# Batch 1's first transform stage in four tiled bursts, its x loads reordered behind the weight scaling, and the swapped-half products moved by 0.8 steps

## The chip, the cores and the metric

One core of a Trainium2 chip runs the whole kernel. The metric is the device time of one execution in microseconds. The kernel before takes 777.56 us (median of three runs, 776.34 to 777.86).

## The reference

```python
def _attn_ref(x, filt_r, filt_i):                 # x: (8, 3008, 256)
    X = np.fft.rfft(x, axis=1)
    Y = X * (filt_r + 1j * filt_i)[None]          # filters: (1505, 256)
    return np.fft.irfft(Y, n=x.shape[1], axis=1)

def _moe_ref(x, w_in, w_out, alpha):              # x: (24064, 256), d_ff 2048
    h = x @ w_in
    g = h + np.sin(alpha * h) ** 2 / (alpha + 1e-09)
    return g @ w_out
```

Each of eight batches is filtered along its 3008 positions with a Fourier transform, and all 24,064 rows then go through a two-layer network with the activation h + sin(alpha h)^2 / alpha.

## The kernel before

**The transform.** 3008 is factored as 47 x 64, and each batch (a `Spectral` object) goes through four matmul stages. The first stage makes 24 complex frequencies of the 47-point transform. A batch's x comes in four pieces (`load_x`, ch 0 to 3), cast to fp16 by the DMA. The results are copied out of PSUM into `t1_h`, stored to DRAM (`d1`, SP queue) and read back turned (`load_t2`, g 0 to 3, GpSimd queue). `forward` (u 0 to 11) multiplies by the table `d_t`, the copy `xf` is made on ScalarE, and the two partition halves of `xf` are swapped into `xs` by two DMAs. `product` multiplies `xf` by the real part of the filter, and `cross` multiplies `xs` by the imaginary part and adds it; both are on VectorE. `inverse` or `inverse_tiled` is the third stage, and `last` the fourth, which leaves the batch in `y`, ready to be the moving operand of the network. Batch 0 has its own code ahead of the main loop; its last pieces (`last_0`) are spread between the matmuls of the main loop.

**Two forms of the first stage.** Batch 1 uses `first(i)`, sixteen matmuls of 94 rows by 512 columns, one PSUM bank each from the pool `fps` (two banks). Batches 2 to 7 use `first_tiled(ch)`: eight matmuls of 47 rows with 64 output columns, which share the array four at a time, fill two banks of `fps` and two of `hps` (four banks, shared with the network's first layer), and are copied out by two passes on ScalarE and two on VectorE. Such a group of eight is called a burst here. `inverse_tiled(w)` is a burst too, of sixteen matmuls.

**The network.** The positions go through in 48 chunks of 512 (the sixth of every twelve has 384). `hidden(k, jb)` makes one tile: two matmuls into one bank of `hps` (line 601), a cosine on ScalarE (line 605), and one combining pass on VectorE that frees the bank (line 606). `project(k, u)` is eight matmuls of 256 columns (line 621) on chunk k's finished tiles; two such halves complete 128 output rows, and every 256 rows are copied by ScalarE to `o` (line 630) and stored by several DMAs from the GpSimd queue (line 665).

**What sets the order.** The program order on every engine is written out by hand. The main loop runs in steps: step s issues two hidden tiles of one chunk, then `slot(s)`, then one or none or two `project` halves of the chunk before, then `slot(s + 0.5)`. `put(at, fn)` lists a piece of transform work with the step it is due at, and a slot runs everything that is due. So a piece due at 8.5 runs after step 8's projection, and one due at 48.3 runs in slot 48.5. Chunk 0 is projected in steps 8 to 15, and its second half of output rows is copied and stored after step 15's projection. `clear` moves forward and last pieces away from a burst, and `aside` moves a product or cross that is due up to 1.1 steps before a burst to just behind it; both know the bursts from the list `bursts`. A DMA that is put in a slot is issued by its engine's queue in this order, and an issue that waits holds everything behind it on that queue.

```python
    def slot(at):
        run = 0
        while pending and pending[0][0] <= at:
            if pending[0][2]:
                if run and pending[0][0] > at - 1:
                    break
                run += 1
            _, _, _, fn, args = pending.pop(0)
            fn(*args)
```

**GpSimd's own work at the start.** It scales the weights: `weights_in` (six pieces, line 542) and `weights_out` (three, line 574), with batch 1's x loads between them (line 168).

Of the kernel before, what the change touches and what calls it, by code (L numbers as in the profile page):

```python
# [10 lines left out]
FP32 = mybir.dt.float32  # L11
# [7 lines left out]
B, S, C = 8, 3008, 256  # L19
# [4 lines left out]
NK = 4 * NS  # L24
FUSED = 1
TILED = 2
# [45 lines left out]
def kernel(  # L72
# [10 lines left out]
    nc = tc.nc  # L83
# [15 lines left out]
    def after(ins, other):  # L99

        tc.add_manual_dep(ins.ins, other.ins.name, mybir.DependencyInfo(
            mybir.DependencyClass.Sync, mybir.DependencyReason.DATA), reason="order of loads")

    def pool(name, bufs, space=None):
        kw = {} if space is None else {"space": space}
        return ctx.enter_context(tc.tile_pool(name=name, bufs=bufs, **kw))
# [11 lines left out]
    fps = pool("fps", 2, PSUM)  # L118
# [3 lines left out]
    wf_t = cpool.tile([NR, NK], FP16)  # L122
    wt_t = cpool.tile([128, 64], FP16)
    wh_t = cpool.tile([NK, NR], FP16)
    t1_h = [cpool.tile([128, 16, C], FP16, name=f"t1_h{i}") for i in range(2)]
# [13 lines left out]
    for h in range(2):  # L139
        nc.sync.dma_start(out=x32[:, 4 * C * h:4 * C * h + 4 * C],  # L140
                          in_=bass.AP(tensor=x.tensor, offset=x.offset + 4 * h * C, ap=[[32 * C, 96], [1, 4 * C]]))
# [12 lines left out]
    marks = {}  # L154

    def load_x(b, ch):
        xt = xpool.tile([128, 8, C], FP16, name=f"x_{b}_{ch}", tag="x")
        if b >= TILED:
            for h in range(2):
                ins = nc.gpsimd.dma_start(  # L160
                    out=xt[64 * h:64 * h + N1],
                    in_=bass.AP(tensor=x.tensor, offset=x.offset + (b * S + 32 * h + ch * 8) * C,
                                ap=[[64 * C, N1], [1, 8 * C]]))
                after(ins, marks["snake"])
            return xt
        xt = xt[0:NR]
        for n0, n in [(0, 8)] if b or ch < 3 else [(0, 4), (4, 4)]:
            ins = nc.gpsimd.dma_start(
                out=xt[:, n0:n0 + n],
                in_=bass.AP(tensor=x.tensor, offset=x.offset + (b * S + ch * 8 + n0) * C,  # L170
                            ap=[[32 * C, NR], [C, n], [1, C]]),
            )
        if b == 0:
            marks["x", ch] = ins
        if b == 1:
            marks["x1", ch] = ins
            after(ins, marks["w_in"])
        return xt

    flip = [0]  # L180
# [1 line left out]
    def evac(dst, src, on_act=None):  # L182
        flip[0] = (flip[0] + 1) % 3
        if flip[0] if on_act is None else on_act:
            marks["act"] = nc.scalar.copy(out=dst, in_=src)  # L185
        else:
            marks["dve"] = nc.vector.tensor_copy(out=dst, in_=src)  # L187

    class Spectral:
# [10 lines left out]
        def load_x(self, ch):  # L200
            self.x[ch] = load_x(self.b, ch)

        def first(self, i):
            ch, j = divmod(i, 4)
            ps = fps.tile([128, 512], FP32, name=f"pa_{self.b}_{i}", tag="f")
            marks["pe"] = nc.tensor.matmul(out=ps[0:NK, :], lhsT=wf_t, rhs=self.x[ch][:, 2 * j:2 * j + 2, :],  # L206
                                           start=True, stop=True)
            r0 = 8 * (ch % 2)
            evac(t1_h[ch // 2][0:NK, r0 + 2 * j:r0 + 2 * j + 2, :], ps[0:NK, :])
            if j == 3:  # L210
                nc.sync.dma_start(out=self.d1_rows[:, 8 * ch:8 * ch + 8, :], 
                                  in_=t1_h[ch // 2][0:NK, r0:r0 + 8, :])

        def first_tiled(self, ch):
            r0 = 8 * (ch % 2)
            for q in range(2):
                own, tag = (hps, "h") if q else (fps, "f")
                ps = [own.tile([128, 512], FP32, name=f"pa_{self.b}_{ch}_{q}_{h}", tag=tag) for h in range(2)]
                for h in range(2):
                    for c in range(2):  # L220
                        n = 4 * c + 2 * q
                        nc.tensor.matmul(out=ps[h][64 * c:64 * c + 64, :], lhsT=wt_t[64 * h:64 * h + N1],  # L222
                                         rhs=self.x[ch][64 * h:64 * h + N1, n:n + 2, :], start=True, stop=True)
                for h in range(2):
                    evac(t1_h[ch // 2][:, r0 + 4 * h + 2 * q:r0 + 4 * h + 2 * q + 2, :], ps[h], h == 0)
            d1 = self.d1.rearrange("a (h n) c -> a h (n c)", h=2)
            for c in range(2):
                n0 = (8 * ch + 4 * c) * C
                nc.sync.dma_start(out=d1[:, :, n0:n0 + 4 * C],
                                  in_=t1_h[ch // 2][64 * c:64 * c + 2 * NS, r0:r0 + 8, :]  # L230
                                  .rearrange("a (h n) c -> a h (n c)", h=2))
# [125 lines left out]
    for g in range(2):  # L357
        gs = slice(12 * g, 12 * g + 12)
        for k, filt in enumerate((filt_r, filt_i)):
            for q in range(2):  # L360
                if (g, k, q) == (0, 1, 1):
                    split_alpha()
                off, step = ((12 * g) * C, C) if q == 0 else ((N1 - 12 * g) * C, -C)
                marks["filt", g, k] = nc.gpsimd.dma_start(
                    out=f_t[k][64 * k + 32 * q:64 * k + 32 * q + 32, gs, :],
                    in_=bass.AP(tensor=filt.tensor, offset=filt.offset + off,
                                ap=[[N1 * C, 32], [step, 12], [1, C]]))
# [88 lines left out]
    for i in range(16):  # L456
        own, tag = (fps, "f") if i % 3 == 2 else (hps, "h")
        ps = own.tile([128, 512], FP32, name=f"pa_0_{i}", tag=tag)
        nc.tensor.matmul(out=ps, lhsT=wf0_t[0:NR], rhs=x0[i // 4][:, 2 * (i % 4):2 * (i % 4) + 2, :],  # L459
                         start=True, stop=True)  # L460
# [60 lines left out]
    for g in range(6):  # L521
        own, tag = (t2pool, "t2") if g < 3 else (gpool, "g")
# [3 lines left out]
        ins = nc.sync.dma_start(out=w_in32[g][1], in_=w_in_v[:, :, js])  # L526
# [8 lines left out]
    for jb in range(0, 16, 8):  # L535
        ins = nc.sync.dma_start(out=w_out32[:, jb:jb + 8],
                                in_=moe_w_out[128 * jb:128 * jb + 1024].rearrange("(b p) c -> p b c", p=128))
    s1 = Spectral(1)
# [37 lines left out]

    spread_alpha(2)
    spread_alpha(3)
    for step in ([(weights_in, g) for g in range(3)] + [(s1.load_x, 0), (weights_in, 3), (s1.load_x, 1),
                 (weights_in, 4), (s1.load_x, 2), (weights_in, 5), (s1.load_x, 3)]  # L580
                 + [(weights_out, jb) for jb in (0, 4, 8)]):
        step[0](*step[1:])
    warm_pe(12)
    last_0(0, 4)
# [86 lines left out]
    def put(at, fn, *args, pe=False):  # L671
        pending.append((at, len(pending), pe, fn, args))

    def firsts(b):

        return {2: (37.5, 39.5, 41.5, 43.5), 3: (49.5, 54.5, 60.5, 66.5)}.get(
            b, [48 * b - 105.5 + 8 * ch for ch in range(4)])

    def inverses(b):

        return (63.5, 73.5, 81.5) if b == 2 else [48 * b - 46.5 + 16 * w for w in range(3)]

    bursts = [at for b in range(TILED, B) for at in (*firsts(b), *inverses(b))]

    def clear(at):

# [2 lines left out]
    def aside(at):  # L689

        return next((s + 0.05 for s in bursts if s - 1.1 < at <= s), at)
# [4 lines left out]
    for jb in range(12, 16):  # L696
        put(5 + 0.5 * (jb - 12), weights_out, jb, 1)

    for n0, n, at in ((6, 5, 1.5), (11, 4, 11), (15, 4, 13), (19, 4, 15.5), (23, 4, 17), (27, 5, 19)):
        put(at, last_0, n0, n, fps, "f", True)  # L700
    for b in range(1, B):
        s = s1 if b == 1 else Spectral(b)
        z = 48 * b
        if b > 1:
            for ch in range(4):
                put(22 + 4 * ch if b == 2 else firsts(b)[ch] - 8, s.load_x, ch)
        if b < TILED:
            for i in range(16):
                put(6.9 + 0.35 * i, s.first, i, pe=True)
        else:  # L710
            for ch in range(4):
                put(firsts(b)[ch], s.first_tiled, ch, pe=True)
        for g in range(4):
            put(12.5 if b == 1 else 45 if b == 2 else max(70, z - 77 + 12 * g), s.load_t2, g)
        for u in range(12):
            inv = 24 + 1.21 * u if b == 1 else 57 + 2.2 * u if b == 2 else z - 59 + 4 * u
            fwd = inv - 6
            fwd = clear(fwd)
            put(fwd, s.forward, u, pe=True)
            put(aside(fwd + (0.5 if b == 1 else 1.5)), s.product, u)  # L720
            if s.fused:
                put(aside(fwd + (4 if b == 1 else 4.5)), s.cross, u)
            if b < TILED:
                put(inv, s.inverse, u, pe=True)
        if b >= TILED:
            for w in range(3):
                put(inverses(b)[w], s.inverse_tiled, w, pe=True)
        for ch in range(4):
            put(z - (9.5 if b == 1 and ch < 3 else (10.5, 10.5, 10.5, 3)[ch]), s.load_t4, ch)
        for u in range(16):  # L730
            put(clear(z + (u - (5 if b == 1 else 6.5) if u < 4 else 2 * u - 9 if b == 1 else 2.6 * u - 11)),
                s.last, u, pe=True)
# [15 lines left out]
    step = 0  # L748
# [43 lines left out]
```

## Time and profile before

| What | Value |
|---|---|
| Median of three runs | 777.56 us (776.34 to 777.86) |
| The profiled execution's own time | 774.94 us |
| Its span, first to last instruction | 773.2 us |
| TensorE busy, matmuls | 762.8 us, 99% |
| VectorE busy | 658.5 us, 85% |
| ScalarE busy | 610.5 us, 79% |
| GpSimd busy | 370.2 us, 48% |
| Combining passes (line 606) | 768, 672 ns each |
| Cosines (line 605) | 768, 599 ns each |
| Copies of first-stage results on VectorE (128x512 and other forms) | 52, 683 ns each |
| Network first layer, 512 columns (line 601) | 1536, 375 ns each |
| Network second layer, 256 columns (line 621) | 3008, 273 ns each |

The duration of a matmul is its own latency; the matmuls overlap, so what one costs is the distance between the starts of two that follow each other. An engine's idle time is followed in the profile by the one that ended it. The names in the profile leave out the buffer numbers: `ph` is a hidden tile's bank, `v` its combined result, `po` a projection, `pa` a first-stage bank, `pb` a forward, `pc` an inverse, `pd` a last stage, `t<-d` is `load_t2`.

### The profile page before, as it was taken

Reading aid. Unit: us, or ns where it says so; the run is one execution under the profiler, and the core shown is the slowest. Engines: PE = TensorE matmul, PEld = TensorE weight load, DVE = VectorE, ACT = ScalarE, POOL = GpSimd, SP = SyncE. Lnnn points to the kernel's source line nnn. Section 1 sums busy time; section 2 is a strip of 40 time slices with the busy share of each in tenths; the row PEclk is TensorE's granted clock in tenths of the full one; section 3 lists DMA queues with packets and bytes.
Section 4 is the critical chain, followed back from the end, with each engine's and each line's share of the span. In section 5 each row is a group of like instructions: output and inputs, shape, how many; then the busy total and the mean of one; then the engine's idle time right before and its main releaser. Section 6 shows DMA issues by size and latency. Waiting matters only on the chain.

```text
span 773.2 us, 17230 instructions
## 1 busy us (share of the span) xinstructions
PE 762.8 (99%) x6039; PEld 517.1 (67%) x6039; DVE 658.5 (85%) x1174; ACT 610.5 (79%) x1204; POOL 370.2 (48%) x649
## 2 busy tenths in 40 slices
PE   8999999999999999999999999999999999999997
PEld 4757766666666666666666666766666666766666
DVE  7886998999989888898889988899888888777774
ACT  6798887898788878888778787888778777777763
POOL 6455455644646555555565647554554645330000
PEclk9999999999999999999999999999999999999999
DMA  9955678854855438554574536764254322511112
GB/s 227 286 104 165 140 161 249 216 138 109 216 143 137 117 71 222 139 119 120 114 200 110 140 93 151 198 149 121 72 146 106 92 70 55 138 45 34 40 36 62
DMA packets 81518, 101.49 MB, mean 131 GB/s; under 512 B 18884, under 2 KB 60864, under 8 KB 81431
## 3 DMA queue, kind: packets, MB, share of 16 engines
q0 software_dynamic: 27440, 47.29, 26.2%
q1 hardware_dynamic: 53503, 52.84, 25.7%
q8 instruction: 47, 0.77, 0.4%
q14 instruction: 40, 0.33, 0.1%
q10 hardware_dynamic: 488, 0.27, 0.1%
HBM read 56.15 MB, written 46.66 MB: 133 GB/s over the span
## 4 chain that ended last, share of the span: by engine, by line
PE 92%; DVE 5%; ACT 1%; issue 1%; DMA 1%; DVEq 0%
PE po L621 41%; PE ph L601 40%; DVE v L606 3%; PE pd L316 2%; PE pb L243 2%; PE pa L222 2%; PE pc L293 1%; PE pc L513 1%; ACT cos_all L605 1%; PE warm L437 1%; PE pb L491 1%; DMA cos_all<-in_x_dram 1%; PE pa L206 0%; PE pd L403 0%; PE pa L459 0%
## 5 line engine op out<-in xcount | busy, mean ns | idle before, releaser
L606 DVE SCALAR_TENSOR_TENSOR v<-cos_all,ph 128x512 f16<-128x512 f32 (+1 forms) x768 | 483.0, 672 | 95.6 <-ACT cos_all L605 92.0
L605 ACT ACTIVATE cos_all<-ph 128x512 f32<-128x512 f32 (+1 forms) x768 | 413.7, 599 | 99.5 <-PE ph L601 98.9
L665 POOL DMA_DIRECT2D out_dram<-o x530 | 291.7, 556 | 244.8 <-ACT o L630 213.5
L601 PE MATMUL ph<-y,w 128*128 128x512 f16 (+1 forms) x1536 | 389.1, 375 | 1.3 <-DVE v L606 1.1
L621 PE MATMUL po<-w,v 128*128 128x256 f16 x3008 | 389.4, 273 | 0.0
L621 PEld LDWEIGHTS <-v 128*128 128x128 f16 x3008 | 290.0, 98 | 84.2 <-issue 1.0
L601 PEld LDWEIGHTS <-w 128*128 128x128 f16 x1536 | 143.1, 98 | 114.0 <-issue 19.1
L630 ACT COPY o<-po 128x512 f32<-128x512 f32 (+1 forms) x95 | 56.1, 590 | 7.8 <-PE po L621 7.5
L246 ACT CAST xf<-pb 128x512 f16<-128x512 f32 x84 | 50.9, 606 | 1.6 <-PE pb L243 0.8
L185 ACT CAST y<-pd 128x376 f16<-128x376 f32 (+1 forms) x86 | 41.9, 490 | 12.2 <-PE pd L316 8.8
L160 POOL DMA_DIRECT2D x<-in_x_dram x48 | 25.6, 538 | 39.4 <-DVE v L606 29.7
L185 ACT CAST t_h<-pa 128x512 f16<-128x512 f32 (+1 forms) x60 | 32.8, 589 | 12.5 <-PE pa L222 11.3
L316 PEld LDWEIGHTS <-t_a 96*128 96x128 f16 x448 | 31.4, 97 | 12.7
L264 DVE TENSOR_TENSOR p<-p,xs 128x512 f16<-128x512 f16 x84 | 35.7, 425 | 2.9
L263 DVE TENSOR_TENSOR xs<-xs,filt_t 128x512 f16<-128x512 f16 x84 | 35.2, 419 | 1.8 <-DMA xs<-xf 1.6
L257 DVE TENSOR_TENSOR p<-xf,filt_t 128x512 f16<-128x512 f16 x84 | 35.1, 419 | 0.0
L185 ACT CAST gt<-pc 128x512 f16<-128x512 f32 x54 | 28.1, 594 | 8.4 <-PE pc L293 8.4
L187 DVE CAST t_h<-pa 128x512 f16<-128x512 f32 (+1 forms) x52 | 33.5, 683 | 0.1
L243 PE MATMUL pb<-t,d_t 128*128 128x256 f16 x168 | 32.1, 273 | 0.0
L316 PE MATMUL pd<-wh_t,t_a 96*128 96x94 f16 x384 | 31.8, 204 | 0.0
L235 POOL DMA_DIRECT2D t<-d x28 | 24.4, 874 | 11.2 <-DMA d<-t_h 10.1
L243 PEld LDWEIGHTS <-d_t 128*128 128x128 f16 x168 | 16.3, 98 | 14.3
(70 smaller groups left out, 276.9 us busy)
## 6 DMA issues: line engine op xcount, KB each, us to landing
t<-d POOLq DMA_DIRECT2D x28, 384.0 KB, 5.2
xs<-xf SPq DMA_DIRECT2D x168, 64.0 KB
t_a<-d SPq DMA_DIRECT2D x28, 384.0 KB
x<-in_x_dram POOLq DMA_DIRECT2D x50, 188.0 KB, 4.8
d<-t_h SPq DMA_DIRECT2D x48, 192.0 KB
d<-gt SPq DMA_DIRECT2D x36, 256.0 KB
out_dram<-o POOLq DMA_DIRECT2D x91, 64.0 KB, 2.1
out_dram<-o POOLq DMA_DIRECT2D x31, 80.0 KB, 3.4
```

The source lines that it names most:

```text
L185: marks["act"] = nc.scalar.copy(out=dst, in_=src)
L243: nc.tensor.matmul(out=ps[:, i, :], lhsT=d_t[:, s, :], rhs=self.t2[s // 6][:, s % 6, :], start=True, stop=True)
L246: nc.scalar.copy(out=self.xf[u], in_=ps)
L263: nc.vector.tensor_tensor(out=xs, in0=xs, in1=f_t[1][:, 2 * u:2 * u + 2, :], op=ALU.mult)
L264: nc.vector.tensor_tensor(out=p, in0=p, in1=xs, op=ALU.add)
L316: nc.tensor.matmul(out=psv[:, i, :], rhs=wi_t if self.b < TILED else wh_t, start=True, stop=True, lhsT=t4_h[ch // 2][0:NK, n0 % 16 + i, cb ...
L601: nc.tensor.matmul(out=ps[:, 0:n], lhsT=w1[:, cb, jb * 128:jb * 128 + 128], rhs=y_cols[:, cb, c0:c0 + n], start=(cb == 0), stop=(cb == 1))
L605: nc.scalar.activation(out=cs[:, 0:n], in_=ps[:, 0:n], func=AFT.Sin, bias=float(np.pi / 2))
L606: marks["snake"] = nc.vector.scalar_tensor_tensor(out=v[k][:, jb, 0:n], in0=cs[:, 0:n], scalar=-1.0, in1=ps[:, 0:n], op0=ALU.add, op1=ALU. ...
L621: nc.tensor.matmul(out=pso[k][:, t % 2, :], lhsT=v[k][:, jb, 128 * t:128 * t + 128], rhs=w2[:, jb, :], start=(jb == 0), stop=(jb == 15))
L630: copy(out=o[:, i0:t % 2 + 1, :], in_=pso[k][:, i0:t % 2 + 1, :])
L665: queues[i % len(queues)].dma_start(out=bass.AP(tensor=out.tensor, offset=out.offset + t0 * C, ap=[*ap, [1, C]]), in_=o_blk[p0:p0 + rows, :])
```

## The change

Batch 1 takes the tiled form, so that `first` is now what `first_tiled` was and the old `first` is gone. Its four bursts are due at steps 8.5, 9.5, 11.5 and 12.5 (before: sixteen single matmuls from 6.9 to 12.15), and they are entered in `bursts`. Its x is loaded by two DMAs a piece, piece 0 behind three `weights_in`, piece 1 behind all six, and pieces 2 and 3 behind the three `weights_out`. Batch 1's `load_t2` is due at 15.5, 16, 18.5 and 21 (before: all at 12.5), batch 2's at 46.5, 49, 53 and 59 (before: all at 45), and one x load of batch 3 at 45 (before 46.5). Five groups of `last_0` get other times. For batches 3 to 7 `cross` is due 5.3 steps behind its forward instead of 4.5.

```diff
     def load_x(b, ch):
         xt = xpool.tile([128, 8, C], FP16, name=f"x_{b}_{ch}", tag="x")
-        if b >= TILED:
+        if b > 0:
             for h in range(2):
...
-                after(ins, marks["snake"])
+                after(ins, marks["w_in" if b == 1 else "snake"])
...
-        def first(self, i):
-            ch, j = divmod(i, 4)
-            ps = fps.tile([128, 512], FP32, name=f"pa_{self.b}_{i}", tag="f")
-            marks["pe"] = nc.tensor.matmul(out=ps[0:NK, :], lhsT=wf_t, rhs=self.x[ch][:, 2 * j:2 * j + 2, :],
-                                           start=True, stop=True)
...
-        def first_tiled(self, ch):
+        def first(self, ch):
...
-    for step in ([(weights_in, g) for g in range(3)] + [(s1.load_x, 0), (weights_in, 3), (s1.load_x, 1),
-                 (weights_in, 4), (s1.load_x, 2), (weights_in, 5), (s1.load_x, 3)]
-                 + [(weights_out, jb) for jb in (0, 4, 8)]):
+    for step in ([(weights_in, g) for g in range(3)] + [(s1.load_x, 0)] + [(weights_in, g) for g in range(3, 6)]
+                 + [(s1.load_x, 1)] + [(weights_out, jb) for jb in (0, 4, 8)] + [(s1.load_x, 2), (s1.load_x, 3)]):
...
-        return {2: (37.5, 39.5, 41.5, 43.5), 3: (49.5, 54.5, 60.5, 66.5)}.get(
+        return {1: (8.5, 9.5, 11.5, 12.5), 2: (37.5, 39.5, 41.5, 43.5), 3: (49.5, 54.5, 60.5, 66.5)}.get(
...
-    bursts = [at for b in range(TILED, B) for at in (*firsts(b), *inverses(b))]
+    bursts = [at for b in range(1, B) for at in (*firsts(b), *(inverses(b) if b >= TILED else ()))]
...
-    for n0, n, at in ((6, 5, 1.5), (11, 4, 11), (15, 4, 13), (19, 4, 15.5), (23, 4, 17), (27, 5, 19)):
+    for n0, n, at in ((6, 5, 1.5), (11, 4, 10.4), (15, 4, 13.2), (19, 4, 14.4), (23, 4, 15.6), (27, 5, 16.8)):
...
-                put(22 + 4 * ch if b == 2 else firsts(b)[ch] - 8, s.load_x, ch)
-        if b < TILED:
-            for i in range(16):
-                put(6.9 + 0.35 * i, s.first, i, pe=True)
...
+                put(22 + 4 * ch if b == 2 else 45 if (b, ch) == (3, 1) else firsts(b)[ch] - 8, s.load_x, ch)
+        for ch in range(4):
+            put(firsts(b)[ch], s.first, ch, pe=True)
         for g in range(4):
-            put(12.5 if b == 1 else 45 if b == 2 else max(70, z - 77 + 12 * g), s.load_t2, g)
+            put((15.5, 16, 18.5, 21)[g] if b == 1 else (46.5, 49, 53, 59)[g] if b == 2 else max(70, z - 77 + 12 * g), s.load_t2, g)
...
-                put(aside(fwd + (4 if b == 1 else 4.5)), s.cross, u)
+                put(aside(fwd + (4 if b == 1 else 4.5 if b == 2 else 5.3)), s.cross, u)
```

More of the change, by code (lines that the diff above doesn't have):

```diff
@@ L163, in load_x @@
                                 ap=[[64 * C, N1], [1, 8 * C]]))
-                after(ins, marks["snake"])
+                after(ins, marks["w_in" if b == 1 else "snake"])
+            if b == 1:
+                marks["x1", ch] = ins
             return xt
         xt = xt[0:NR]
-        for n0, n in [(0, 8)] if b or ch < 3 else [(0, 4), (4, 4)]:
+        for n0, n in [(0, 8)] if ch < 3 else [(0, 4), (4, 4)]:
             ins = nc.gpsimd.dma_start(
@@ L172, in load_x @@
             )
[L173 to L177, printed above, removed]
+        marks["x", ch] = ins
         return xt
@@ L201, in load_x @@
             self.x[ch] = load_x(self.b, ch)
-        def first(self, i):
-            ch, j = divmod(i, 4)
-            ps = fps.tile([128, 512], FP32, name=f"pa_{self.b}_{i}", tag="f")
-            marks["pe"] = nc.tensor.matmul(out=ps[0:NK, :], lhsT=wf_t, rhs=self.x[ch][:, 2 * j:2 * j + 2, :],
-                                           start=True, stop=True)
[L208 to L212, printed above, removed]
-        def first_tiled(self, ch):
+        def first(self, ch):
             r0 = 8 * (ch % 2)
@@ L705 @@
             for ch in range(4):
-                put(22 + 4 * ch if b == 2 else firsts(b)[ch] - 8, s.load_x, ch)
-        if b < TILED:
-            for i in range(16):
-                put(6.9 + 0.35 * i, s.first, i, pe=True)
-        else:
-            for ch in range(4):
-                put(firsts(b)[ch], s.first_tiled, ch, pe=True)
+                put(22 + 4 * ch if b == 2 else 45 if (b, ch) == (3, 1) else firsts(b)[ch] - 8, s.load_x, ch)
+        for ch in range(4):
+            put(firsts(b)[ch], s.first, ch, pe=True)
         for g in range(4):
-            put(12.5 if b == 1 else 45 if b == 2 else max(70, z - 77 + 12 * g), s.load_t2, g)
+            put((15.5, 16, 18.5, 21)[g] if b == 1 else (46.5, 49, 53, 59)[g] if b == 2 else max(70, z - 77 + 12 * g), s.load_t2, g)
         for u in range(12):
```

## The prediction

> **What bounds the kernel now.** I read the page's engine list and chain first, then busy time by stretch, to see where TensorE (PE) is not full.
>
> ```profile
> PE 762.8 (99%) x6039; PEld 517.1 (67%) x6039; DVE 658.5 (85%) x1174; ACT 610.5 (79%) x1204; POOL 370.2 (48%) x649
> ...
> PE 92%; DVE 5%; ACT 1%; issue 1%; DMA 1%; DVEq 0%
> ```
>
> ```profile
> 46.00:65.06 19.06, 18.43 (x128) 12.38 (x127) 14.19 (x24) 16.65 (x33) 4.76 (x8) 1.00 0.35 99
> 65.06:81.70 16.64, 16.20 (x134) 12.48 (x132) 13.55 (x26) 13.24 (x26) 11.37 (x20) 1.00 0.53 151
> 81.70:98.50 16.80, 16.80 (x125) 12.00 (x124) 16.60 (x36) 15.57 (x32) 7.09 (x15) 1.00 0.71 153
> ```
>
> The first numbers are the stretch, its length and PE's busy time. From step 24 (81.7 us) on PE has no room: what the change takes off PE's work is gained there, what it makes PE wait is lost, and speeding any other engine is worth nothing. Between steps 8 (46.0) and 24 some PE time is idle. So I followed PE's sequence, and asked of each wait which queue ends it.
>
> Prices: the chain shows eight matmuls of 512 columns in 1.73 us (0.216 each) and eight of 256 in 0.88 (0.110). A step of four and eight is thus 1.74 us. A last-stage matmul between them costs 0.04 (starts 73.49 and 73.53 below).
>
> **The first stage.** Sixteen matmuls of 0.216 go (3.46 us). A burst takes 0.56 (batch 4's: eight from 328.13, next hidden tile at 328.69), so four are 2.24: PE's work shrinks by 1.2. In steps 8 to 15 (45.99 to 65.06) PE had 8 x 1.74 + 14 x 0.216 + 16 x 0.04 = 17.6 us of work in 19.1, so waits of 1.5. The new order has 13.95 + 2.24 + 24 x 0.04 = 17.15, and VectorE takes eight copies at 0.61 from start to start where it had four. Two bursts in successive steps then give it 2 x 1.22 + 2 x 1.22 = 4.9 us against PE's 4.6, and the third burst's second `fps` bank must wait until VectorE has copied `pd_11_1`, which stands behind two combining passes (some 1.0 us). Following the four `hps` and two `fps` banks by hand from 45.7, when the passes free step 8's first bank, I get step 16 at 64.65, with waits of 1.8. Bounds are no wait at all (62.8) and twice as much (66.5). Eight more last-stage matmuls are then behind it (0.3). **Term 1: -0.7 us** (-2.5 to +1.1).
>
> The x loads: piece 0 as before (34.45); three `weights_in` (1.76, 1.79, 1.23) end at 40.4, piece 1 at 41.5, `weights_out` (5.59) at 47.1, as before, and pieces 2 and 3 are issued by 48.2 and 49.3. Landing took 4.5 to 6.3 us there, so 53.1 and 55.5, against bursts at 54.8 and 58.2. The cover is 1.7 us and costs nothing; if it is gone, PE waits by what is missing. Eight stores to `d1` instead of four (0.33 of SP's time each) have an idle SP queue.
>
> **`load_t2` of batch 1** is the largest single step. Before, it stood ahead of the second group of output stores; at 15.5 it is behind them. That group waits for the copy after step 15's projection:
>
> ```profile
> 56.15 3.69 POOL L665 DMA_DIRECT2D out_dram<-o  x7 [9.07 <-ACT o L630]
> 65.62 3.34 POOL L235 DMA_DIRECT2D t<-d  x4 [5.79 <-DMA d<-t_h]
> 68.95 2.65 POOL L665 DMA_DIRECT2D out_dram<-o  x5
> ```
>
> ```profile
> 65.26 0.59 ACT L630 COPY o<-po 128x512 f32<-128x512 f32 x1 [0.22 <-PE po L621]
> ```
>
> ```profile
> 70.06 0.38 PE L243 MATMUL pb<-t,d_t 128*128 128x256 f16 x2
> ```
>
> Before, GpSimd waited for `d1` until 65.62, the first load landed 4.0 us later (69.62), and forward 0 ran at 70.06 without a wait. Call the start of step 16 R (65.06 before). The copy ends at R + 0.8, the stores begin 0.3 later (55.86 to 56.15 in the first group), seven take 3.69, the load follows at R + 4.8 and lands at R + 8.8; `d1` is complete long before. PE needs from R two steps, two hidden tiles and sixteen last-stage matmuls: 3.49 + 0.86 + 0.64 = 5.0. It reaches forward 0 at R + 5.0 and stands until R + 8.8, and in-order behind that are the projections. **Term 2: +3.8** (3.0 to 4.6, by landings of 4.0 and issue times of 0.5). [...] The other loads are needed four and more steps later.
>
> A wait of before goes: at step 20 PE stood for a bank,
>
> ```profile
> 73.49 0.20 PE L403 MATMUL pd<-wi_t,t_a 128*128 128x94 f16 x1
> 73.53 0.38 PE L601 MATMUL ph<-y,w 128*128 128x512 f16 x1
> 74.35 0.20 PE L403 MATMUL pd<-wi_t,t_a 128*128 128x94 f16 x1 [0.43 <-ACT xf L246]
> ```
>
> 0.82 between the last two starts instead of 0.22. That last stage now comes ahead of forward 0. **Term 3: -0.6** (-0.6 to 0).
>
> **Batch 2's `load_t2` and batch 3's x load: 0.** The first load was issued at 130.26, when `d1` had landed; at 46.5 GpSimd still comes before that. It landed at 134.4 and forward 0 of batch 2 is due at 135.6: that margin covers it. The others come later by less than the steps they have.
>
> **Cross 0.8 later.** Slots run at halves, so 4.5 and 5.3 are one whole step apart: in VectorE's queue the two passes (0.8 us together) move from in front of a step's two combining passes to behind them. PE gains nothing, since VectorE's waits for `xs` (1.6 us in all) did not reach it. It can lose at a burst: the banks that a burst takes leave PE only one step ahead of VectorE. The move puts cross exactly between the two steps ahead of every `inverse_tiled` of batches 3 to 7. Batch 2 shows that case today, cross and product ahead of the last passes before its burst at 180.60:
>
> ```profile
> 179.55 0.42 DVE L263 TENSOR_TENSOR xs<-xs,filt_t 128x512 f16<-128x512 f16 x1
> 180.00 0.43 DVE L264 TENSOR_TENSOR p<-p,xs 128x512 f16<-128x512 f16 x1
> 180.35 0.42 DVE L257 TENSOR_TENSOR p<-xf,filt_t 128x512 f16<-128x512 f16 x1
> 180.68 1.28 DVE L606 SCALAR_TENSOR_TENSOR v<-cos_all,ph 128x512 f16<-128x512 f32 x2
> ```
>
> ```profile
> 181.41 1.19 PE L601 MATMUL ph<-y,w 128*128 128x512 f16 x4 [0.19 <-DVE v L606]
> ```
>
> The next hidden tiles wait 0.4 us in all (181.41 for 181.16, and 1.03 becomes 1.19). Batch 3's first burst before:
>
> ```profile
> 224.79 0.42 DVE L263 TENSOR_TENSOR xs<-xs,filt_t 128x512 f16<-128x512 f16 x1
> 225.24 0.42 DVE L264 TENSOR_TENSOR p<-p,xs 128x512 f16<-128x512 f16 x1
> 225.92 2.59 DVE L606 SCALAR_TENSOR_TENSOR v<-cos_all,ph 128x512 f16<-128x512 f32 x4 [0.26 <-ACT cos_all L605]
> ```
>
> The four passes start at 225.92, held by a cosine. With cross behind the second of them (227.13), the third starts at 227.93 and the fourth ends at 229.2; PE wanted the fourth's bank at 228.80: 0.4 lost. Read the same way, fifteen bursts give 4 x 0.43, 2 x 0.75 (batches 4 and 6, w = 0, behind a step without projection), 3 x 0.3 and 6 x 0.05 = 4.4 us. At first-stage bursts cross and product now stand together two steps ahead; where a last-stage copy is beside them (seven of sixteen) 0.2 to 0.5 is lost, 2.5 together. Each of these is a difference of 0.05 to 0.5 between starts, so I take all of the first and less than half of the second. **Term 4: +5.5** (0 to +8; a gain of 1.0 at most, the waits at 319.5 and 503.3).
>
> **Sum.** -0.7 - 0.6 + 3.8 + 5.5 = +8.0. The profiled execution (774.94 us: span 773.2, 1.7 around it) would come to 782.9; it lies 2.6 below the median, so I add to the median: 777.56 + 8.0 = **785.6 us**. About 0.2% (1.6 us) is what a measurement can tell from no change.
>
> **Rivals.**
> Cross is free (0.22): where it lands VectorE has enough slack after all, as the six bursts at 0.05 nearly have; against it stands the wait at 181.41. Terms 1 to 3 alone: 777.56 + 2.5 = 780.1.
>
> Forward 0 doesn't wait (0.18): the load reaches PE in time although it is behind the stores. It decides at R + 5.0, so stores and landing must be 3.8 faster than their rows. For it: spans on GpSimd are called rough in the page. Against: two groups of seven took 3.69 and 3.59. With cross free too, -0.7 - 0.6 gives 776.3; with no wait in steps 8 to 15 either, -3.1, 774.5. This is the side of no change or faster.
>
> A cold restart (0.08): at the start, PE's first ten warm-up matmuls took 4.45 us, 0.43 apart, twice the later 0.216. A stop of 3.8 us, when 1.1 is the longest before, could bring that back: ten at the double price, +2.1, 787.7. [...]
>
> **Chances and range.** Forecast 0.52, cross free 0.22, no wait 0.18, cold restart 0.08. From forecast, cross free and cold restart: slower 0.80 (780.1 is 0.3% slow; a little of it falls short). The no-wait case divides into 0.12 faster and 0.06 same, and 0.02 of the cross-free case is same. Low end: the best first stage and cross free, -2.5 - 0.6 + 3.0 = -0.1, so 777.5. High: terms 2 and 4 at their upper ends and the others at their values, -0.7 + 4.6 - 0.6 + 8 = +11.3, give 788.9; with part of the cold restart's 2.1 I set 790.0.
>
> **What would show it.** PE: a wait of 3 to 4.6 us at the first `pb` of batch 1, ended by the DMA of `t<-d`, whose issue follows seven stores; step 16 near 64.7; waits of `ph` for `v` behind `pc` bursts, 0.4 each, near 0.75 at batches 4 and 6. I am wrong if forward 0 runs within 1 us of its turn, or if PE stays gapless from step 24 on.

## The result, and the profile after

| | Before | After |
|---|---|---|
| Median of five runs | 777.56 us (776.34 to 778.33) | 786.63 us (785.69 to 787.47) |
| The profiled execution's own time | 774.94 us | 787.47 us |
| Its span | 773.2 us | 785.7 us |
| Mean granted TensorE clock | 0.999 | 0.996 |

The change makes the kernel slower, by a ratio of 1.0119 (95% interval 1.0099 to 1.0138), 9.07 us between the medians. The two profiled executions lie 12.5 us apart, because the one before is 2.6 below its median and the one after 0.8 above; where the traces are compared below, the differences are therefore larger than those of the medians. In the kernel after, some lines have other numbers: a hidden tile's matmuls are L587, its cosine L591, its combining pass L592, a projection L607, its copy L616, its store L651, a burst of the first stage L209, `load_t2` L222, a forward L230, `cross` L250 and L251, `inverse_tiled` L280, a last stage of batch 0 L390.

The engine list and the chain of the page after:

```profile
PE 767.9 (98%) x6055; PEld 518.1 (66%) x6055; DVE 658.0 (84%) x1178; ACT 612.0 (78%) x1200; POOL 372.8 (47%) x653
...
PE 84%; DVE 8%; ACT 4%; issue 2%; DMA 1%; POOL 0%; ACTq 0%; POOLq 0%; DVEq 0%
```

The matmuls' busy time rose by 5.1 us and their number by 16 (the four bursts have 32 where there were 16 single ones), and on the chain VectorE and ScalarE went from 6% to 12%: the chain leaves TensorE more often, for an engine that held a matmul up. The same stretches as before tell where. Busy time by stretch, after, cut at the starts of steps 0, 16 and 24 and at the end (columns: stretch, length, busy time of PE, PEld, DVE, ACT and POOL with the number of instructions, granted clock, DMA share, GB/s):

```profile
36.35:65.46 29.11, 27.52 (x196) 16.59 (x195) 25.93 (x43) 24.86 (x49) 16.66 (x19) 1.00 0.58 127
65.46:87.53 22.07, 18.66 (x128) 13.07 (x127) 13.68 (x25) 13.04 (x26) 11.49 (x20) 0.85 0.42 111
87.53:785.70 698.17, 690.54 (x5432) 466.82 (x5429) 588.33 (x1072) 549.46 (x1084) 326.52 (x580) 1.00 0.49 123
```

The kernel before, cut at the same steps, for the first and the last of the three:

```profile
35.93:65.06 29.13, 27.79 (x172) 17.17 (x171) 23.16 (x39) 26.03 (x52) 14.80 (x16) 1.00 0.55 118
...
81.72:773.20 691.48, 686.72 (x5432) 465.59 (x5429) 591.33 (x1072) 546.58 (x1084) 326.02 (x580) 1.00 0.50 124
```

The first stage changed nothing (29.11 against 29.13). Steps 16 to 23 took 22.07 us where before they took 16.66, and in them the granted clock was 0.85. The rest took 698.17 against 691.48 for the same 5432 matmuls; of these 6.7 us PE is called busy for 3.8 (690.54 against 686.72), so more than half of the loss doesn't appear as idle time at all.

Steps 16 to 23 hold the single largest wait. The chain of waits after, from 65.6 on (columns: start, duration, engine, what):

```profile
65.63 0.57 ACT o L616
...
66.49 2.67 POOL out_dram L651 x6
69.56 0.39 POOL out_dram L651
70.08 3.90 DMA t<-d
74.03 0.61 PE pb L230 x2
```

The copy of step 15's projection, seven stores on the GpSimd queue, `load_t2` issued behind them at 70.08, its landing 3.9 us later, and then forward 0 of batch 1: each link is one that the prediction named. PE's timeline at that place, after:

```profile
70.20 0.38 PE L587 MATMUL ph<-y,w 128*128 128x512 f16 x1
74.03 0.61 PE L230 MATMUL pb<-t,d_t 128*128 128x256 f16 x2 [3.41 <-DMA t<-d]
...
76.30 1.91 PE L587 MATMUL ph<-y,w 128*128 128x512 f16 x4
79.92 1.03 PE L587 MATMUL ph<-y,w 128*128 128x512 f16 x4
```

Four matmuls of a hidden step lasted 1.91 us at 76.30 and 1.03 at 79.92: behind the wait PE ran at half speed. Busy time by stretch around it, after (the column after POOL's is the granted clock):

```profile
70.62:72.87 2.25, 0.00 (x1) 0.00 (x0) 1.29 (x2) 0.81 (x2) 2.00 (x3) 1.00 0.58 176
72.87:74.03 1.16, 0.00 (x0) 0.00 (x1) 0.00 (x0) 0.00 (x0) 0.00 (x0) 0.50 1.01 198
74.03:79.69 5.66, 5.66 (x24) 3.52 (x25) 2.35 (x4) 1.78 (x3) 0.00 (x0) 0.50 0.43 129
79.69:81.00 1.31, 1.31 (x10) 0.78 (x8) 0.00 (x0) 1.09 (x3) 0.22 (x1) 1.00 0.00 0
```

The clock fell at 72.87, 2.25 us after the last matmul had ended, and came back at 79.69, 5.66 us after PE had work again. In all it was down for 6.82 us.

The loss behind step 24 is spread over the bursts. PE's timeline at the first burst of `inverse_tiled` of batches 3 and 4, after:

```profile
233.96 0.63 PE L280 MATMUL pc<-p,e_t 64*64 64x256 f16 x16
234.64 1.19 PE L587 MATMUL ph<-y,w 128*128 128x512 f16 x4
...
325.58 0.51 PE L280 MATMUL pc<-p,e_t 64*64 64x256 f16 x9
326.71 0.41 PE L280 MATMUL pc<-p,e_t 64*64 64x256 f16 x7 [0.62 <-DVE p L251]
327.31 1.19 PE L587 MATMUL ph<-y,w 128*128 128x512 f16 x4 [0.19 <-DVE v L592]
```

From the burst's start to the next hidden tile it is 0.68 us in batch 3 and 1.73 in batch 4, where a burst that nothing holds takes 0.56. (Batch 4's takes 0.94 without the move of `cross` too, in both_back below, so 0.79 of it is new.) In batch 3 no wait is listed at all; the four hidden matmuls last 1.19 instead of 1.04. The list of PE's waits behind step 24, after (engine, what, whom it waited for: us in all, times, longest):

```profile
PE ph L587 <- DVE v L592: 1.1, 6, 0.2
PE pc L280 <- DVE p L251: 1.1, 2, 0.6
```

It counts 2.2 us, where the same list of the kernel before has 0.6, of a loss of 6.4 to 6.7. What holds the banks is VectorE's order, here in its timeline after:

```profile
231.91 1.28 DVE L592 SCALAR_TENSOR_TENSOR v<-cos_all,ph 128x512 f16<-128x512 f32 x2 [0.88 <-ACT cos_all L591]
233.12 0.42 DVE L250 TENSOR_TENSOR xs<-xs,filt_t 128x512 f16<-128x512 f16 x1
233.57 0.43 DVE L251 TENSOR_TENSOR p<-p,xs 128x512 f16<-128x512 f16 x1
233.91 1.28 DVE L592 SCALAR_TENSOR_TENSOR v<-cos_all,ph 128x512 f16<-128x512 f32 x2
```

The two passes of `cross` stand between the combining passes of the two steps ahead of the burst at 233.96, as forecast, and the second pair starts 0.79 us later (233.91 for 233.12).

### The profile page after: what moved, and what is told of

It is laid out like the page before. It is cut to its first block, busy times and chain, and to the rows that moved or that the text cites. A ratio compares the mean times of both kernels' runs of the same rounds, so it can differ in the third digit from the quotient of the medians.

```text
span 785.7 us, 17270 instructions
## 1 busy us (share of the span) xinstructions
PE 767.9 (98%) x6055; PEld 518.1 (66%) x6055; DVE 658.0 (84%) x1178; ACT 612.0 (78%) x1200; POOL 372.8 (47%) x653
## 4 chain that ended last, share of the span: by engine, by line
PE 84%; DVE 8%; ACT 4%; issue 2%; DMA 1%; POOL 0%; ACTq 0%; POOLq 0%; DVEq 0%
PE ph L587 37%; PE po L607 37%; DVE v L592 5%; PE pd L303 2%; PE pb L230 2%; ACT cos_all L591 2%; PE pa L209 2%; DVE p L251 1%; DVE xs L250 1%; PE pc L500 1%; DMA w<-in_moe_alpha_dram 1%; ACT t_h L183 1%; PE pc L280 1%; PE warm L424 1%; PE pb L478 1%
## 5 line engine op out<-in xcount | busy, mean ns | idle before, releaser
L592 DVE SCALAR_TENSOR_TENSOR v<-cos_all,ph 128x512 f16<-128x512 f32 (+1 forms) x768 | 480.7, 672 | 105.3 <-ACT cos_all L591 102.9
L591 ACT ACTIVATE cos_all<-ph 128x512 f32<-128x512 f32 (+1 forms) x768 | 413.3, 596 | 104.4 <-PE ph L587 100.8
L651 POOL DMA_DIRECT2D out_dram<-o x530 | 291.8, 557 | 255.8 <-ACT o L616 228.0
L587 PE MATMUL ph<-y,w 128*128 128x512 f16 (+1 forms) x1536 | 392.6, 375 | 2.9 <-DVE v L592 1.7
L607 PE MATMUL po<-w,v 128*128 128x256 f16 x3008 | 391.2, 273 | 0.0
L607 PEld LDWEIGHTS <-v 128*128 128x128 f16 x3008 | 290.9, 98 | 84.7 <-issue 1.0
L587 PEld LDWEIGHTS <-w 128*128 128x128 f16 x1536 | 144.0, 98 | 117.9 <-issue 25.6
L616 ACT COPY o<-po 128x512 f32<-128x512 f32 (+1 forms) x95 | 55.0, 579 | 8.5 <-PE po L607 7.8
L160 POOL DMA_DIRECT2D x<-in_x_dram x56 | 29.7, 536 | 45.5 <-DVE v L592 33.0
L183 ACT CAST t_h<-pa 128x512 f16<-128x512 f32 x56 | 30.2, 590 | 13.2 <-PE pa L209 13.2
L251 DVE TENSOR_TENSOR p<-p,xs 128x512 f16<-128x512 f16 x84 | 35.7, 425 | 2.9
L185 DVE CAST t_h<-pa 128x512 f16<-128x512 f32 x56 | 35.9, 684 | 0.5 <-PE pa L209 0.4
L230 PE MATMUL pb<-t,d_t 128*128 128x256 f16 x168 | 32.3, 274 | 3.4 <-DMA t<-d 3.4
L250 DVE TENSOR_TENSOR xs<-xs,filt_t 128x512 f16<-128x512 f16 x84 | 35.2, 419 | 0.2 <-DMA xs<-xf 0.2
L230 PEld LDWEIGHTS <-d_t 128*128 128x128 f16 x168 | 16.4, 98 | 18.0 <-DMA t<-d 3.7
L185 DVE CAST y<-pd 128x376 f16<-128x376 f32 (+2 forms) x42 | 22.7, 543 | 4.4 <-PE pd L390 4.4
```

What stands on the lines that cost most here:

```text
L230: nc.tensor.matmul(out=ps[:, i, :], lhsT=d_t[:, s, :], rhs=self.t2[s // 6][:, s % 6, :], start=True, stop=True)
L251: nc.vector.tensor_tensor(out=p, in0=p, in1=xs, op=ALU.add)
L587: nc.tensor.matmul(out=ps[:, 0:n], lhsT=w1[:, cb, jb * 128:jb * 128 + 128], rhs=y_cols[:, cb, c0:c0 + n], start=(cb == 0), stop=(cb == 1))
L591: nc.scalar.activation(out=cs[:, 0:n], in_=ps[:, 0:n], func=AFT.Sin, bias=float(np.pi / 2))
L592: marks["snake"] = nc.vector.scalar_tensor_tensor(out=v[k][:, jb, 0:n], in0=cs[:, 0:n], scalar=-1.0, in1=ps[:, 0:n], op0=ALU.add, op1=ALU. ...
L607: nc.tensor.matmul(out=pso[k][:, t % 2, :], lhsT=v[k][:, jb, 128 * t:128 * t + 128], rhs=w2[:, jb, :], start=(jb == 0), stop=(jb == 15))
```

## The experiments

All stretches, in one table: lengths in us between the starts of steps 0, 8, 16, 24 and 72 and the end of the last matmul, from one profiled execution each, and the median of all runs, with its ratio to the kernel before run on the same chip.

| Kernel | 0–8 | 8–16 | 16–24 | 24–72 | 72–end | Median | Ratio (95%) |
|---|---|---|---|---|---|---|---|
| before | 10.06 | 19.07 | 16.67 | 95.31 | 592.02 | 777.56 | |
| after | 9.80 | 19.31 | 22.07 | 95.30 | 598.43 | 786.63 | 1.0119 (1.0099–1.0138) |
| cross_back | 9.79 | 19.32 | 20.81 | 95.30 | 592.71 | 781.37 | 1.0045 (1.0028–1.0062) |
| t2_ahead | 9.80 | 19.31 | 15.76 | 95.83 | 598.43 | 781.40 | 1.0056 (1.0036–1.0075) |
| both_back | 9.78 | 19.32 | 15.76 | 95.30 | 592.33 | 775.93 | 0.9989 (0.9977–1.0001) |
| before_cross | 10.05 | 19.06 | 17.50 | 95.37 | 598.43 | 782.74 | 1.0069 (1.0047–1.0092) |
| u3_back | 9.80 | 19.31 | 22.10 | 95.30 | 594.08 | 783.19 | 1.0083 (1.0066–1.0100) |
| keep_warm | 9.80 | 19.31 | 19.52 | 95.56 | 598.38 | 785.74 | 1.0119 (1.0104–1.0134) |
| before_t2 | 10.07 | 19.07 | 23.06 | 95.30 | 592.01 | 782.18 | 1.0065 (1.0048–1.0082) |
| last_later | 9.80 | 18.20 | 16.54 | 95.30 | 592.72 | 775.74 | 0.9982 (0.9967–0.9997) |

The time ahead of step 0 is left out: it varied from 35.9 to 38.5 us between executions.

**cross_back: the changed kernel without the move of `cross`.**

```diff
-                put(aside(fwd + (4 if b == 1 else 4.5 if b == 2 else 5.3)), s.cross, u)
+                put(aside(fwd + (4 if b == 1 else 4.5)), s.cross, u)
```

> The changed kernel with cross of batches 3 to 7 due 4.5 steps behind its forward again. Theory (each cross pair now delays the combining passes in front of a burst, and PE, full from step 24 on, waits): the stretch from step 24 to the end falls from 698.2 us back to 691.5, the time from 786.6 to 779.9. Rival (the longer stretch comes from elsewhere, for example the moved loads): the stretch stays at 698 and the time at 786.6.

The last stretch fell from 598.43 to 592.71 and the stretch of `load_t2` kept its wait, so the two losses are separate. The median is 4.5 us above the kernel before beside it, where after's was 9.1. PE's timeline at forward 0, cross_back:

```profile
74.94 0.49 PE L230 MATMUL pb<-t,d_t 128*128 128x256 f16 x2 [3.23 <-DMA t<-d]
```

Busy time by stretch behind it, cross_back:

```profile
75.11:78.52 3.41, 3.41 (x16) 2.08 (x15) 0.98 (x2) 0.92 (x2) 0.00 (x0) 0.50 0.71 211
```

Here the clock was down for 3.41 us only, half of after's 6.82, behind a wait of nearly the same length; that is most of what steps 16 to 23 took less (20.81 against 22.07).

**t2_ahead: the changed kernel with batch 1's loads due at 12.5 again.**

```diff
-            put((15.5, 16, 18.5, 21)[g] if b == 1 else (46.5, 49, 53, 59)[g] if b == 2 else max(70, z - 77 + 12 * g), s.load_t2, g)
+            put(12.5 if b == 1 else (46.5, 49, 53, 59)[g] if b == 2 else max(70, z - 77 + 12 * g), s.load_t2, g)
```

> The changed kernel with batch 1's load_t2 due at 12.5 again, so ahead of the second group of output stores. Theory (the loads stood behind seven stores, and PE's stop then let the clock fall): no wait at forward 0, granted clock 1.00 in steps 16 to 24, this stretch 22.1 us to about 16, the time 786.6 to about 780.7. Rival (the stores to d1 are what is late, eight DMAs instead of four): forward 0 still waits 2 us or more and the clock may still fall, 783 to 786.

GpSimd's timeline, t2_ahead:

```profile
66.63 3.33 POOL L222 DMA_DIRECT2D t<-d  x4 [6.13 <-DMA d<-t_h]
69.95 2.67 POOL L651 DMA_DIRECT2D out_dram<-o  x5
```

PE's timeline, t2_ahead:

```profile
71.03 0.38 PE L230 MATMUL pb<-t,d_t 128*128 128x256 f16 x2
```

Busy time by stretch, steps 16 to 23, t2_ahead:

```profile
66.00:81.76 15.76, 15.76 (x127) 11.85 (x126) 13.39 (x25) 12.83 (x26) 11.42 (x20) 1.00 0.55 159
```

With the loads ahead of the stores, forward 0 has no wait, the clock stays at 1.00, and the stretch is PE's work alone, 15.76 of 15.76. That is 6.31 less than after: 3.41 of the wait and 2.9 of the half clock behind it. It is also 0.91 less than in the kernel before, which is the gain of the re-timed last stages. The last stretch stays at 598.43: it depends on `cross` alone.

**both_back: both of these edits.**

> The changed kernel with both cross (4.5) and batch 1's load_t2 (12.5) as before: the tiled first stage, its x loads and the moved last stages alone. Theory (the two losses add, and the first stage is worth the eight last-stage matmuls and the wait at step 20): 1 us under the kernel before, about 776.6. Rival (the losses overlap, one hides in the other): the sum of the two single gains, about 12 us, is not reached, 779 or more.

Nothing of the loss is left: 592.33 in the last stretch, 15.76 in steps 16 to 23, and a ratio of 0.9989 (0.9977 to 1.0001). So all else that the change does, the four bursts among it, is worth 0.9 us by the medians, and by the interval something between 1.8 us and nothing.

**before_cross and before_t2: the two parts alone, on the kernel before.** They show whether a part needs the rest of the change to do harm. before_cross:

```diff
-                put(aside(fwd + (4 if b == 1 else 4.5)), s.cross, u)
+                put(aside(fwd + (4 if b == 1 else 4.5 if b == 2 else 5.3)), s.cross, u)
```

> The kernel before with cross of batches 3 to 7 due at 5.3 instead of 4.5, nothing else. Theory (cross alone costs what the changed kernel loses from step 24 on): 777.6 + 6.7 = 784.3, with waits of ph at the inverse bursts. Rival (cross costs only together with the other moves): 777.6.

before_t2:

```diff
-            put(12.5 if b == 1 else 45 if b == 2 else max(70, z - 77 + 12 * g), s.load_t2, g)
+            put((15.5, 16, 18.5, 21)[g] if b == 1 else 45 if b == 2 else max(70, z - 77 + 12 * g), s.load_t2, g)
```

> The kernel before with batch 1's load_t2 due at 15.5, 16, 18.5 and 21, nothing else: single first-stage matmuls as before. Theory (the place behind the seven stores alone makes the wait): a wait of 3.3 to 3.8 us at forward 0 and up to 2.7 of half clock behind it, the wait of 0.6 at step 20 gone, steps 16 to 24 in 19.5 to 22.3 us instead of 16.7, 777.2 + 3 to 5.5 = 780 to 783. Rival (the wait needs the later x loads or the two-part d1 stores): 777.2.

PE's timeline at the first inverse burst of batch 4, before_cross, where the inverse is L293 and a hidden tile L601:

```profile
322.26 0.41 PE L293 MATMUL pc<-p,e_t 64*64 64x256 f16 x7 [0.62 <-DVE p L264]
322.86 1.19 PE L601 MATMUL ph<-y,w 128*128 128x512 f16 x4 [0.19 <-DVE v L606]
```

These two waits are those of after, to the hundredth, and the last stretch is 598.43 again: 6.41 us more than before. The median rose by 5.9. In steps 16 to 23 this execution took 0.83 more than before, with a wait of 0.7 for batch 1's load; as the move doesn't touch batch 1, that is not put down to `cross`; what made it isn't shown.

PE's timeline and the clock, before_t2:

```profile
74.41 0.61 PE L243 MATMUL pb<-t,d_t 128*128 128x256 f16 x2 [3.39 <-DMA t<-d]
```

```profile
65.85:88.90 23.05, 19.25 (x134) 13.81 (x132) 13.74 (x26) 13.46 (x26) 11.47 (x20) 0.85 0.40 109
```

A wait of 3.39 and a clock of 0.85: the same loss without the tiled first stage. The median rose by 5.4 us. One part of the expectation missed: the wait at step 20 stayed, since the last stages are where they were, and the stretch, 23.05 us, lies above the 19.5 to 22.3 that were expected. The line of that wait, before_t2:

```profile
81.53 0.20 PE L403 MATMUL pd<-wi_t,t_a 128*128 128x94 f16 x1 [0.41 <-ACT xf L246]
```

The two parts are thus causes by themselves, and additive to within 1.3 us: 5.9 and 5.4 alone, less 0.9 of both_back, make 10.4 where the whole change measured 9.1.

**u3_back: which bursts `cross` disturbs.** In the changed kernel, only each fourth `cross`, the one in the two steps ahead of an inverse burst, goes back to 4.5:

```diff
-                put(aside(fwd + (4 if b == 1 else 4.5 if b == 2 else 5.3)), s.cross, u)
+                put(aside(fwd + (4 if b == 1 else 4.5 if b == 2 or u % 4 == 3 else 5.3)), s.cross, u)
```

> The changed kernel with cross due at 4.5 again only for u = 3, 7 and 11 of batches 3 to 7 (15 of 60), those directly ahead of an inverse burst. Theory (what costs is a cross one step ahead of an inverse burst, and less so two steps ahead of a first-stage burst): the waits behind pc at steps 97 to 305 go, about 4.2 of the 6.4 us lost behind step 72, and 2.2 stay at first-stage bursts: 786.6 - 4.2 = 782.4. Rival (every late cross costs the same): a quarter of 6.4 comes back, 785.0.

The last stretch fell from 598.43 to 594.08: 4.35 of the loss are the fifteen inverse bursts, caused by a quarter of the moved products. PE's timeline at the same first bursts of batches 3 and 4, u3_back:

```profile
234.29 0.63 PE L280 MATMUL pc<-p,e_t 64*64 64x256 f16 x16
234.86 1.04 PE L587 MATMUL ph<-y,w 128*128 128x512 f16 x4
...
325.23 0.74 PE L280 MATMUL pc<-p,e_t 64*64 64x256 f16 x16
326.16 1.19 PE L587 MATMUL ph<-y,w 128*128 128x512 f16 x4 [0.19 <-DVE v L592]
```

Batch 3's burst is back at 0.57 (234.29 to 234.86) and the four matmuls at 1.04. In batch 4 the wait within the burst is gone, and the burst takes 0.93 (325.23 to 326.16), as in both_back. The remaining 1.4 us (594.08 less the 592.71 of cross_back) to 2.1 (less the 592.02 of before) belong to the other three quarters.

**keep_warm: work for PE during the wait.** In the changed kernel fifteen matmuls on weights are issued ahead of forward 0; their result isn't used.

```diff
+    def fill_pe(n):
+        ps = hps.tile([128, 512], FP32, name="fill", tag="h")
+        for i in range(n):
+            nc.tensor.matmul(out=ps, lhsT=d_t[:, 0, :], rhs=w1[:, 0, 0:512], start=True, stop=True)
+
+    put(17.99, fill_pe, 15)
```

> The changed kernel with fifteen matmuls of 512 columns (3.2 us, their result is not used) put directly ahead of batch 1's forward 0, where PE stands 3.6 us for the load. Theory (the stop of PE is what lets the clock fall): forward 0 runs at the same time, granted clock 1.00 in steps 16 to 24, that stretch 22.1 us to about 19.4, the time up to 2.7 under the changed kernel, about 784. Rival (the slow matmuls behind forward 0 come from the transfers that land then, not from the stop): the stretch stays at 22 and the clock at 0.5.

PE's timeline, keep_warm:

```profile
72.57 3.40 PE L683 MATMUL fill<-w,d_t 128*128 128x512 f16 x15
76.34 0.39 PE L230 MATMUL pb<-t,d_t 128*128 128x256 f16 x2 [0.37 <-DMA t<-d]
77.53 1.03 PE L587 MATMUL ph<-y,w 128*128 128x512 f16 x4
```

Busy time by stretch, keep_warm, behind the filling and at the start of the kernel:

```profile
76.00:87.08 11.08, 10.74 (x80) 7.76 (x81) 8.12 (x16) 8.20 (x16) 5.36 (x10) 1.00 0.54 144
...
5.30:8.63 3.33, 1.59 (x7) 0.58 (x6) 2.77 (x4) 0.65 (x1) 1.20 (x2) 1.00 1.06 210
8.63:12.04 3.41, 3.36 (x8) 1.13 (x8) 1.56 (x3) 1.22 (x2) 2.42 (x8) 0.50 1.08 273
```

The load landed as late as before (forward 0 began 8.8 us behind the start of step 16, in after 8.6), PE could still not begin forward 0, and yet steps 16 to 23 took 19.52 instead of 22.07: the clock stayed at 1.00, and 2.55 us came back. That part of the loss is therefore the clock and not the wait. The whole time hardly shows it (median 0.9 lower, the same ratio), for two reasons. This execution, at 787.19 us the longest of four, ran at half clock for 3.41 us at its start instead, from 8.63 on; the other three have clocks of 0.999 and 1.000 and take 785.01 to 785.85. And the restart doesn't come in every execution: the five of after have mean clocks of 0.996, 0.998, 0.999, 0.997 and 0.997 at 787.47, 786.34, 785.69, 786.63 and 787.27 us. The one with 0.999 is the fastest.

**last_later: both_back with the last stages of batch 0 at other times.** In the first stage a wait was left at the third burst: from its first matmul to the next hidden tile it takes 1.75 us (55.30 to 57.05) where 0.56 would do, so 1.19 are lost. PE's timeline, after:

```profile
55.30 0.40 PE L209 MATMUL pa<-x,wt_t 47*64 47x512 f16 x2
56.49 0.62 PE L209 MATMUL pa<-x,wt_t 47*64 47x512 f16 x6 [0.79 <-ACT t_h L183]
```

Two copies end near 56.49, one on ScalarE and one on VectorE, in their timelines after:

```profile
55.85 0.59 ACT L183 CAST t_h<-pa 128x512 f16<-128x512 f32 x1
55.99 0.54 DVE L185 CAST y<-pd 128x376 f16<-128x376 f32 x1
```

The expectation below takes VectorE's copy of the last-stage bank `pd_11_1` for the one that the burst waits for. By the times it can't be: it ends at 56.53, 0.04 behind the matmul that goes on at 56.49, while the ScalarE copy that the profile names ends at 56.44. That one copies the burst's own first bank. In the program that is built from the changed kernel both `fps` tiles of this burst stand in one bank, and `pd_11_1` in the other, so the third matmul has to wait until ScalarE has emptied what the first two filled. Either way the last stages just ahead of the burst are at fault, and moving them away must take the wait away:

```diff
-    for n0, n, at in ((6, 5, 1.5), (11, 4, 10.4), (15, 4, 13.2), (19, 4, 14.4), (23, 4, 15.6), (27, 5, 16.8)):
+    for n0, n, at in ((6, 5, 1.5), (11, 4, 12.9), (15, 4, 13.9), (19, 4, 14.9), (23, 4, 15.9), (27, 5, 16.9)):
```

> The changed kernel with cross and batch 1's load_t2 as before, and the five moved groups of last_0 at 12.9, 13.9, 14.9, 15.9 and 16.9, so that none lies ahead of the third first-stage burst. Theory (the wait of 1.0 us inside that burst is for VectorE's copy of pd_11_1 out of an fps bank): steps 8 to 16 fall from 19.3 to 18.3 us, the work then behind step 16 grows by 0.2 to 0.4, 775.2, 1.5 to 2 under the kernel before. Rival (the burst waits for its x, which comes later, or the wait moves to the next bank): 775.9.

PE's timeline at the third burst, last_later:

```profile
56.51 0.63 PE L209 MATMUL pa<-x,wt_t 47*64 47x512 f16 x8
57.07 1.04 PE L587 MATMUL ph<-y,w 128*128 128x512 f16 x4
```

The burst runs in one piece (in this program its two `fps` tiles stand in two banks) and steps 8 to 15 take 18.20 instead of 19.32. But 0.78 of the 1.12 came back in steps 16 to 23 (16.54 for 15.76), where the last stages now stand close together and wait for their two banks. At 775.74 us, ratio 0.9982 (0.9967 to 0.9997), this version is 0.2% below the kernel before, less than the 1.5 to 2 us that were expected; the ratio of both_back, 0.9989, lies within that interval, so the two are not told apart.

## Why the prediction was right, by its steps

The forecast was 785.6 us and the median is 786.63. The mechanisms were those forecast, but for the link that held the third burst (term 1); the sizes were off by up to 1 us in both directions, and one rival came true beside the forecast. That the sum came within 1.1 us of the median is in part luck. Between the two profiled executions the stretches from step 0 on lost 11.8 us (5.4 in steps 16 to 23 and 6.4 behind step 72), 3.8 more than the forecast, most of it the slower clock.

**Term 1, the first stage (-0.7, of which -0.4 by step 16).** The stretch from step 0 to 16 gained 0.02. A wait at the third burst, forecast at 1.0, was there with 1.19, but not behind VectorE's copy of `pd_11_1` as the prediction had it: the matmul went on 0.04 before that copy ended, and behind ScalarE's copy of the burst's own first bank. So the size came out near by luck, while the cause, last stages in the `fps` banks ahead of the burst, was right. Steps 0 to 7 gained 0.26, but steps 8 to 15 lost 0.24 where the hand count had them 0.1 shorter. So the matmuls that went were paid for with waits for banks, a little more than was counted. last_later shows that 1.1 us of it hung on the last stages ahead of the third burst.

**Term 2, `load_t2` (+3.8).** The wait was 3.41 in after, 3.23 in cross_back, 3.39 in before_t2 and 3.6 in u3_back. The load was, in after, issued 4.62 us behind the start of step 16 and not 4.8, and landed 3.9 later and not 4.0. The rival "forward 0 does not wait" falls: 3.8 us weren't to be had from stores that GpSimd issues in 3.60 us.

**Term 3, the wait at step 20 (-0.6).** It went. t2_ahead and both_back have 15.76 us where before had 16.67, the 0.6 together with the 0.3 of the last stages that were done earlier.

**Term 4, `cross` (+5.5).** The last stretch lost 5.72 (after less cross_back) to 6.41 (before_cross less before). The inverse bursts were read at 4.4 in all; u3_back gives 4.35. Burst by burst, the time from a burst's first matmul to the end of the next two hidden tiles' issue, after less both_back, is longer by 0.27 to 0.46 at seven bursts, 0.79 and 0.63 at the two of batches 4 and 6 (forecast 0.75 each), and 0.07 to 0.08 at six, 4.3 together. The step that was mis-sized, by the traces, is the discount: of the first-stage bursts' 2.5 "less than half" was taken, 1.1, and 1.4 to 2.1 are there. The rival "cross is free" falls with before_cross.

**The cold restart (chance 0.08, +2.1).** The chance was too low; the price was near: 2.9 us of steps 16 to 23 in after, 2.55 of which keep_warm gave back. After waits of 3.41, 3.23 and 3.39 us the clock fell in the profiled executions of after, cross_back and before_t2, whose steps 16 to 23 have 0.85, 0.92 and 0.85; that of u3_back, with a wait of 3.6, took 22.10 us for these steps and has 0.994 over its whole span. Of all executions of these four kernels (5, 6, 4 and 4), 14 of 19 have a mean clock of 0.998 or less; of those of both_back, t2_ahead, before_cross and last_later, whose profiles have no such wait, 4 of 29. Among the six of cross_back, two have a clock of 0.999 and 1.000 and take 779.2 us, and four have 0.996 or 0.997 and take 781.2 to 781.8, some 2 us more. In the other three kernels the executions at 0.998 or less lie 0.7 to 3.0 us above the single one that is over it, so from whole times the price of a restart is known only roughly. The one execution of after with 0.999 took 785.69, the forecast's own 785.6; the median has the restart in it.

**The sum.** By medians of runs on one chip, `cross` is worth 5.5 us (t2_ahead less both_back), the load 5.4 (cross_back less both_back), and all else -0.9. The forecast had 5.5, 3.8 and -1.3. The largest miss is thus the load's term, 1.6 too low, which holds the restart beside the wait. The three together make 10.0 where the whole change measured 9.1, and what the remaining 0.9 is stays open (the medians are of four to ten executions, and in those with the wait the restart comes or not).

## What to carry to other kernels

A load that the critical engine needs must be placed by everything that its own queue issues ahead of it: seven stores of 0.5 us each were enough to turn a hidden load into a stop of 3.4 us, and with it came a granted clock of 0.50 for 6.82 us in after, 2.9 us more. On a kernel whose TensorE is full, two passes of 0.42 us moved by one step on another engine cost 6 us, because each burst of matmuls takes two of the four `hps` banks and leaves one step's banks in reserve; to price such a move, write out the bank sequence at every burst, and trust small differences that repeat fifteen times. And measure losses by the distance between starts, since the list of waits showed 2.2 us, against 0.6 in the kernel before, of a loss of 6.4.

## What the runs showed of the hardware

Around the stop for batch 1's load the granted clock fell to 0.50, at another moment and for another time in each of the two profiled executions that were cut finely enough to tell. In after it fell 2.25 us after the last matmul had ended, with 1.16 us of the wait still to go, and stayed at 0.50 for 6.82 us, in 5.66 of which PE was at work again. In cross_back the wait of 3.23 us ended at 74.94 with the clock still at 1.00; it fell at 75.11, 0.17 us later, and stayed at 0.50 for 3.41 us, half as long, with PE busy for all 3.41. In before_t2, behind a wait of 3.39 us, it has a mean of 0.85 over the 23.05 us of steps 16 to 23, as in after over 22.07.

The length of a stop alone doesn't decide it in these runs. At the start of keep_warm the clock fell at 8.63, at the end of a wait of 1.11 us and after 3.33 us in which PE was busy for 1.59, again for 3.41 us. last_later stood twice at the same line, 3.4 us in all and 1.7 in the longer stop, and its profiled execution has a mean clock of 1.00. And of the executions of one kernel some keep the clock: one of after's five has 0.999, two of cross_back's six have 0.999 and 1.000. What decides when the clock falls, and for how long, the runs don't show.
